# A Newton iteration for 32x32 inverses: sixteen small array tiles, or one whole array with masked, block-diagonal weights

## The chip, the cores and the metric

The kernel runs on one core of a Trainium2 chip. The metric is device time of one execution in microseconds, lower is better. Engines: TensorE (PE in the profile, PEld for its weight loads), VectorE (DVE), ScalarE (ACT), GpSimd (POOL), SyncE (SP).

## The reference

Nystrom attention on 8 batches of 8 heads (576 tokens, head size 64), then a multiplicative feed-forward layer on the 4608 resulting tokens:

```python
q_lm = q.reshape(B, H, m, S // m, D).mean(axis=3)         # m = 32 landmarks
A, Bm, C = sm(q, k_lm), sm(q_lm, k_lm), sm(q_lm, k)       # softmax of scaled products
Z = Bm.T / (norm1(Bm) * norminf(Bm) + 1e-6)               # per head, 32x32
for _ in range(6):
    Z = 2 * Z - Z @ Bm @ Z                                # iterative inverse
x = (A @ Z @ C @ v)                                       # heads side by side: 4608 x 512
out = ((x @ w1) * (x @ w2)) @ w3 @ w_out                  # 512 -> 1024 -> 1024 -> 512
```

## The kernel before, in words

**Stages.** The product w3 w_out is formed once on the chip (`w34`): w3 comes in eight row blocks of 128, each is turned on TensorE (`w3_tr`, tasks `tr`), split into a high and a low f16 part on ScalarE and VectorE (`w3_hi`, `w3_lo`), and multiplied with the equally split w_out (`w34_mm`, tasks `mm{j}{c}`, three matmuls each). w_out comes in eight pieces (`wf{c}`). Meanwhile the attention runs for "quads" of four heads (`quad_tasks`, sixteen of them): GpSimd loads q and k (`lq`), sums them to landmark means (`mean_a` to `mean_c`), VectorE transposes, TensorE makes the scores (tasks `S`, `A`), and so on. A pair of batches g (four pairs) then goes through the "lane" (`pair_tasks`): softmax of Bm and its norms (`ba` to `no`), five steps of the iteration (`x{g}_{i}`), a last product (`Z`), its spreading to a block-diagonal tile `zb` on VectorE (`z_out`, task `zo`), the product with C v (`W`), a split to f16 (`w_out`, task `wq`), and from there, for each of the two batches, the products with w1 and w2 (`U`). Last come the dense stages: `d` (192 columns, four matmuls of two heads' groups each) with their product on ScalarE and VectorE (`e`, `f`), and `g` (512 columns, four matmuls per task) with copy and store. The dense stages of one batch run on TensorE between the attention work of later ones.

**The iteration.** The tile `xz` holds, for 16 heads, X = I - Bm Z (part 0) and Z (part 1), head hb of four in partitions 32 hb to 32 hb + 31, and four groups s side by side. A step is X times (X, Z): for each of the 16 heads a 32x32 f32 weight tile and 64 moving columns, each at its own 32x32 place of the array (`it_mm`). Then ScalarE copies X X to the next tile (`it_sq`, task `v`), and VectorE adds X Z to Z (`it_out`, task `y`). The next step needs both.

**What sets the order.** `Plan` is a list scheduler that runs while the kernel is built. Each task has an engine, an assumed duration, dependencies, ring buffers that it takes (`acq`) and gives back (`rel`), a due time (`prio`) and for TensorE a mode, the array's tile shape. It starts, engine by engine, the task that can start first; on TensorE tasks within 0.05 us of that compete by due time, and one in the array's present mode has its due time moved ahead, by MP = 0.9 for the whole array and by MT for the small tile shapes. The result is a fixed order for each engine's in-order queue; only semaphores decide when things run. Due times follow from `dense(b) = T0 + 19.5 b`; `att(n)` for quads and `lane(g)` for the iteration are set off from it.

Names and lines that the text uses: line 239 is the helper `mm` (all plain matmuls), 310 the w_out load, 315 the w3 load, 333 the w3 transposes, 415 the q and k loads, 436 the w1 and w2 loads, 452 to 467 the landmark sums on GpSimd, 626 a normalisation on GpSimd, 815 `it_sq`, 824 `it_out`, 839 `z_out`, 859 and 860 `w_out`, 959 and 965 the dense product. `swapneg` is a constant 128x128 f32 matrix with which TensorE exchanges row maxima between partitions (`s_swap`, tasks `sw`). `bank` is any of six PSUM banks; buffers named `osb`, `ecT` and `u` also serve as landing places of weights at the start.

Of the kernel before, what the change touches and what calls it, by code (L numbers as in the profile page):

```python
# [11 lines left out]
ALU = mybir.AluOpType  # L12
AX = mybir.AxisListType

B = 8
# [7 lines left out]
DF = 1024  # L23
HALF = 288
MP = 0.9
MT = 12.0
THIRD = 192
NCH = 8
X64 = 64.0
# [12 lines left out]
class Plan:  # L42
# [15 lines left out]
    def add(self, name, eng, dur, fn, deps=(), acq=(), rel=(), prio=0.0, mode=None, lat=None,  # L58
            move=0.0, after=0.0):
        t = Task(name, eng, dur, fn, list(deps), list(acq), list(rel), prio, mode,  # L60
                 self.LAT[eng] + self.SLACK if lat is None else lat, move, after)
        self.by[name] = t
        self.tasks.append(t)
        return t
# [101 lines left out]
def kernel(  # L166
# [11 lines left out]
    nc = tc.nc  # L178
    P = Plan()
# [7 lines left out]
    def bank(i):  # L187
        return banks[i]
# [28 lines left out]
    xzs = slots(fixed, 3, [128, 4, 2, 32], FP32, "xz")  # L217
# [15 lines left out]
    def at(key, i=0):  # L233
        return P.slot[key][i]
# [3 lines left out]
    def mm(out_, lhsT, rhs, start=True, stop=True, pos=None):  # L238
        nc.tensor.matmul(out_, lhsT, rhs, start=start, stop=stop,  # L239
                         **({} if pos is None else {"tile_position": pos}))  # L240


    T0 = 66.0
    PER = 19.5

    def dense(b):
# [1 line left out]

    def att(n):
        first = dense(2 * (n // 4)) - 53.0 + 7.5 * (n % 4)  # L250
        return max(3.0 + 6.0 * n, first)

    def lane(g):
        return dense(2 * g) - 26.0
# [58 lines left out]
    def load_w3(j, c0=0, c1=DF):  # L313
        def fn():
            nc.sync.dma_start(out=w3n[at(f"w3n{j}")][:, c0:c1], in_=moe_w3[128 * j:128 * j + 128, c0:c1])
        return fn
# [45 lines left out]
    def w34_out(j):  # L362
# [2 lines left out]
                                 scale=1.0 / (WSC * WSC))  # L365
        return fn

    def w34_tasks():
        for j in range(8):
            p0 = 4.0 + 8.6 * j  # L370
            cuts = [(0, 1), (1, 4), (4, 8)] if j == 0 else [(0, 4), (4, 8)]
            acq = [("w3n", f"w3n{j}", 1, len(cuts))]
            if j == 0:
                for h, (c0, c1) in enumerate(cuts):
                    add(f"wm{h}" if h else "w3n0", "SP", 0.43, load_w3(0, 128 * c0, 128 * c1),
                        acq=[] if h else acq, prio=(-0.01, 0.105, 0.115)[h], move=0.183 * (c1 - c0), lat=2.0)
            else:
                add(f"w3n{j}", "SP", 0.43, load_w3(j), acq=acq, prio=0.125 if j == 1 else p0 - 8.0,
                    after=0.0 if j == 1 else max(0.0, p0 - 12.0), move=1.46, lat=2.0)
            if j == 0:  # L380
                for c in range(8):
                    add(f"wf{c}", "SP", 0.43, load_wout(c), acq=[("wf", f"wf{c}", 1, 2)],
                        prio=0.1 + 0.01 * c, move=0.73, lat=2.0)
                    add(f"woh{c}", "ACT", 0.53, wout_hi(c), deps=[f"wf{c}"], rel=[f"wf{c}"],
                        prio=1.0 + 0.1 * c)
                    add(f"wol{c}", "DVE", 0.62, wout_lo(c), deps=[f"wf{c}", f"woh{c}"],
                        rel=[f"wf{c}"], prio=1.0 + 0.1 * c)
            for h, (c0, c1) in enumerate(cuts):
                acq = [("P", f"ptr{j}{h}", 1, 2)]
                if h == 0:  # L390
                    acq.append(("w3t", f"w3t{j}", 1, 8))
                k = (c1 - c0) / 4
                add(f"tr{j}{h}", "PE", 0.44 * k, w3_tr(j, h, c0, c1),
                    deps=["cb", f"wm{h}" if h and j == 0 else f"w3n{j}"] + ([f"tr{j}{h - 1}"] if h else []), acq=acq,
                    rel=[f"w3n{j}"], prio=p0 - 4.0 + h, mode="full")
                add(f"wh{j}{h}", "ACT", 0.13 + 0.35 * k, w3_hi(j, h, c0, c1), deps=[f"tr{j}{h}"], rel=[f"ptr{j}{h}"],
                    prio=p0 - 3.5 + h)
                add(f"wl{j}{h}", "DVE", 0.1 + 0.51 * k, w3_lo(j, h, c0, c1), deps=[f"tr{j}{h}", f"wh{j}{h}"],
                    rel=[f"ptr{j}{h}"], prio=p0 - 3.5 + h)
            part = {c: h for h, (c0, c1) in enumerate(cuts) for c in range(c0, c1)}  # L400
            for c in range(8):
                deps = [f"woh{c}", f"wol{c}", f"wh{j}{part[c]}", f"wl{j}{part[c]}"]
                if c:
                    deps.append(f"mm{j}{c - 1}")
                add(f"mm{j}{c}", "PE", 0.65, w34_mm(j, c), deps=deps,
                    acq=[("P", f"pw{j}", 1, 1)] if c == 0 else [], rel=[f"w3t{j}"],
                    prio=p0 + 0.7 * c, mode="full")
            add(f"wo{j}", "ACT", 0.48, w34_out(j), deps=[f"mm{j}7"], rel=[f"pw{j}"], prio=p0 + 6.0)
# [391 lines left out]
    def it_mm(g, i):  # L800
        def fn():
            ps, xz = bank(at(f"pX{g}_{i}")), xzs[at(f"xz{g}_{i}")]
            for s in range(4):
                for hb in range(4):
                    r = slice(32 * hb, 32 * hb + 32)
                    mm(ps[r, 64 * s:64 * s + 64], xz[r, s, 0, :], xz[r, s, :, :],
                       pos=(32 * hb, 32 * hb))
        return fn

    def it_ps(g, i):  # L810
        return bank(at(f"pX{g}_{i}"))[:, 0:256].rearrange("p (s t x) -> p s t x", s=4, t=2)

    def it_sq(g, i):
        def fn():
            nc.scalar.copy(out=xzs[at(f"xz{g}_{i + 1}")][:, :, 0, :], in_=it_ps(g, i)[:, :, 0, :])  # L815
        return fn
# [10 lines left out]
    def z_mm(g):  # L827
        def fn():
            ps, xz = bank(at(f"pZ{g}")), xzs[at(f"xz{g}_5")]
            for s in range(4):  # L830
                for hb in range(4):
                    r = slice(32 * hb, 32 * hb + 32)
                    mm(ps[r, 32 * s:32 * s + 32], xz[r, s, 1, :], xz[r, s, 0, :],
                       pos=(32 * hb, 32 * hb))
        return fn
# [60 lines left out]
    def pair_tasks(g):  # L896
        p = lane(g)
        add(f"ba{g}", "DVE", 0.5, b_soft_a(g), deps=[f"bo{4 * g + i}" for i in range(4)],
            acq=[("tiny", f"tb{g}", 1, 2), ("P", f"pN{g}", 1, 1)], rel=[f"bsc{g}"], prio=p)
        add(f"bb{g}", "ACT", 0.25, b_soft_b(g), deps=[f"ba{g}"], prio=p + 0.3)  # L900
        add(f"bc{g}", "DVE", 1.08, b_soft_c(g), deps=[f"bb{g}"], acq=[("bm", f"bm{g}", 1, 1)],
            rel=[f"tb{g}"], prio=p + 0.6)
        add(f"N{g}", "PE", 0.52, norm_mm(g), deps=[f"bc{g}"], prio=p + 1.5, mode="32x32")
        add(f"no{g}", "DVE", 1.47, norm_out(g), deps=[f"N{g}"],
            acq=[("xz", f"xz{g}_0", 1, 2)], rel=[f"pN{g}", f"bm{g}", f"tb{g}"], prio=p + 2.0)
        last = [f"no{g}"]
        for i in range(5):
            add(f"x{g}_{i}", "PE", 0.46, it_mm(g, i), deps=last,
                acq=[("P", f"pX{g}_{i}", 1, 1 if i == 4 else 2), ("xz", f"xz{g}_{i + 1}", 1, 1 if i == 4 else 2)],
                rel=[f"xz{g}_{i}"], prio=p + 3.5 + 1.5 * i, mode="32x32")  # L910
            last = [f"y{g}_{i}"]
            add(f"y{g}_{i}", "DVE", 0.44 if i == 4 else 0.22, it_out(g, i), deps=[f"x{g}_{i}"],
                rel=[f"xz{g}_{i}", f"pX{g}_{i}"], prio=p + 3.8 + 1.5 * i)
            if i < 4:
                add(f"v{g}_{i}", "ACT", 0.24, it_sq(g, i), deps=[f"x{g}_{i}"], rel=[f"pX{g}_{i}"],
                    prio=p + 3.8 + 1.5 * i)
                last.append(f"v{g}_{i}")
        add(f"Z{g}", "PE", 0.28, z_mm(g), deps=last, acq=[("P", f"pZ{g}", 1, 1)], rel=[f"xz{g}_5"],
            prio=p + 11.0, mode="32x32")
        add(f"zo{g}", "DVE", 0.6, z_out(g), deps=[f"Z{g}"], acq=[("zb", f"zb{g}", 1, 1)],  # L920
            rel=[f"pZ{g}"], prio=p + 11.3)
        add(f"W{g}", "PE", 0.47, w_mm(g), deps=[f"zo{g}", f"co{2 * g}", f"co{2 * g + 1}"],
            acq=[("P", f"pY{g}", 1, 1)],
            rel=[f"zb{g}", f"cv{2 * g}", f"cv{2 * g + 1}"], prio=p + 12.0, mode="128x64")
        add(f"wq{g}", "DVE", 0.8, w_out(g), deps=[f"W{g}"], acq=[("wT", f"wT{g}", 1, 8)],
            rel=[f"pY{g}"], prio=p + 12.3)

    def u_tasks(b):
        p = dense(b) - UO
# [137 lines left out]
    for s in range(2):  # L1067
        for qd in range(2):
            for wi in range(2):
                add(f"lw{s}{qd}{wi}", "POOL", 0.62, load_w12(s, qd, wi), prio=T0 - 10.0 + qd, after=T0 - 10.0 - 4.0,  # L1070
                    move=1.46, lat=2.0)
    for n in range(NQ):
        quad_tasks(n)
# [54 lines left out]
```

## Time and profile before

| | |
|---|---|
| runs | 283.07 us median of 3 (281.07, 283.07, 283.90) |
| profiled execution | 281.59 us, its span 279.8 us |
| mean granted TensorE clock | 0.997 |
| instructions in the profile | 9998 |
| DMA | 37.34 MB moved, mean 133 GB/s |

The profile is one execution as the hardware profiler took it. Times are us from the span's start. In a line of a group stand: line, engine, operation, output and input tiles, shapes, count; then busy us in total and mean ns of one; then idle time of the engine just before these instructions, and what ended it. In a timeline a line is a run of like instructions: start, us from the first start to the last end, engine, line, operation, tiles, shape, count; in brackets the idle time before it and its releaser. A matmul's end is modelled and overlaps the next one's start, so for TensorE the distance between starts is what counts. One f32 matmul of the program shows as two records. The engines' busy time over the span (40 slices, tenths):

```profile
PE   3799999988999999999999899999999999999993
PEld 1456566744647767776676666756776665775762
DVE  2669995978858999779979757777883462442540
ACT  4643453424467776567986177599746667768551
POOL 8902999987998979989898920121010000000000
```

### The profile page before, as it was taken

What the parts mean: (1) busy time and instruction counts of PE and PEld (TensorE: products, weight loads), DVE (VectorE), ACT (ScalarE), POOL (GpSimd) and SP (SyncE); (2) the same over time, 40 slices, a digit from 0 to 9 for tenths busy, and PEclk for the clock granted to TensorE, in tenths of its full rate; (3) what the DMA queues carried; (4) which work ended last, traced back from release to release, by engine and by line L of the source; (5) the groups of instructions that cost most, each with busy time, mean ns of one, the idle gap of its engine ahead of it and who ended that gap; (6) DMA issues with size and microseconds to landing.
All of it is one profiled execution on the core that took longest, in us unless ns stands there. A gap on an engine that the chain in (4) does not pass through costs nothing.

```text
span 279.8 us, 9998 instructions
## 1 busy us (share of the span) xinstructions
PE 264.4 (94%) x4116; PEld 177.3 (63%) x4116; DVE 195.0 (70%) x514; ACT 167.2 (60%) x457; POOL 141.9 (51%) x183
## 2 busy tenths in 40 slices
PE   3799999988999999999999899999999999999993
PEld 1456566744647767776676666756776665775762
DVE  2669995978858999779979757777883462442540
ACT  4643453424467776567986177599746667768551
POOL 8902999987998979989898920121010000000000
PEclk9999999999999999999999999999999999999998
DMA  6999995999935564789832751211211112121223
GB/s 176 316 316 270 256 286 116 232 219 215 187 66 87 86 124 127 171 234 184 178 98 89 180 156 40 76 39 41 77 41 42 40 45 71 63 89 40 77 76 112
DMA packets 19181, 37.34 MB, mean 133 GB/s; under 512 B 2880, under 2 KB 3392, under 8 KB 19136
## 3 DMA queue, kind: packets, MB, share of 16 engines
q1 hardware_dynamic: 13136, 24.91, 29.3%
q0 software_dynamic: 5760, 11.54, 23.7%
q8 instruction: 32, 0.52, 0.8%
q10 hardware_dynamic: 240, 0.26, 0.3%
q14 instruction: 13, 0.11, 0.1%
HBM read 38.80 MB, written 9.44 MB: 172 GB/s over the span
## 4 chain that ended last, share of the span: by engine, by line
PE 80%; DVE 12%; DMA 2%; issue 2%; ACT 1%; SPq 1%; DVEq 0%
PE bank L239 73%; PE wide L239 4%; DVE ab L965 3%; DMA osb<-in_moe_w_dram 2%; PE bank L333 2%; DVE bank L747 1%; PE bank L635 1%; DVE tiny L598 1%; DVE ea L604 1%; DVE ecT L563 1%; DVE tiny L520 1%; DVE tiny L619 1%; DVE Tq L444 1%; DVE Tk L444 0%; SPq L310 0%
## 5 line engine op out<-in xcount | busy, mean ns | idle before, releaser
L239 PEld LDWEIGHTS <-u 128*128 128x128 f16 x960 | 81.3, 99 | 32.2 <-issue 8.1
L965 DVE TENSOR_TENSOR ab<-asb,bank 128x192 f16<-128x192 f16 x192 | 60.2, 347 | 38.4 <-ACT asb L959 37.9
L239 PE MATMUL bank<-aT,u 128*128 128x192 f16 x768 | 78.2, 247 | 0.3 <-DVE ab L965 0.3
L239 PE MATMUL bank<-w,ab 128*128 128x512 f16 (+1 forms) x296 | 73.4, 374 | 0.8 <-issue 0.8
L959 ACT CAST asb<-bank 128x192 f16<-128x192 f32 x192 | 57.5, 329 | 22.9 <-PE bank L239 19.4
L239 PE MATMUL bank<-wo,u 128*128 128x512 f16 x192 | 50.5, 395 | 0.0
L459 POOL TENSOR_TENSOR ls<-ls 128x128 f32<-128x128 f32 (+2 forms) x56 | 40.8, 728 | 3.6
L239 PEld LDWEIGHTS <-ab 128*128 128x128 f16 x296 | 26.9, 98 | 22.0 <-issue 3.8
L452 POOL TENSOR_TENSOR ls<-nat 128x1152 f32<-128x1152 f16 x14 | 33.3, 2382 | 12.5 <-DVE Tk L444 12.1
L881 ACT CAST u<-bank 128x512 f16<-128x512 f32 x64 | 35.2, 599 | 6.4 <-PE bank L239 6.2
L626 POOL TENSOR_TENSOR ah<-ea,tiny 128x512 f16<-128x512 f32 (+1 forms) x16 | 18.5, 1159 | 37.9 <-ACT u L881 16.5
L991 ACT ACTIVATE osb<-bank 128x512 f32<-128x512 f32 x35 | 21.2, 605 | 12.7 <-PE bank L239 12.5
L547 ACT ACTIVATE ec<-wide,tiny 128x288 f32<-128x288 f32 x32 | 15.8, 501 | 9.1 <-DVE tiny L540 9.0
L239 PE MATMUL bank<-w,wT 64*32 64x512 f16 x512 | 18.9, 380 | 0.0
L239 PE MATMUL bank<-vb,ecT 128*32 128x128 f32 x576 | 17.9, 273 | 0.0
L340 ACT ACTIVATE u<-bank 128x512 f16<-128x512 f32 (+2 forms) x17 | 9.7, 569 | 12.2 <-PE bank L333 8.5
L467 POOL TENSOR_TENSOR lm<-ls,meanS 128x256 f16<-128x256 f32 x28 | 16.6, 617 | 0.4
L239 PE MATMUL bank<-xz 32*32 32x64 f32 (+1 forms) x768 | 15.1, 213 | 1.6 <-DVE cv L737 1.4
L239 PEld LDWEIGHTS bank<-xz 32*32 32x32 f32 x768 | 11.2, 105 | 7.5 <-issue 2.4
L815 ACT COPY xz<-bank 128x128 f32<-128x128 f32 x16 | 4.3, 269 | 19.3 <-PE bank L239 19.1
L239 PEld LDWEIGHTS bank<-vb,ecT 128*32 128x32 f32 x576 | 15.7, 110 | 0.3 <-issue 0.2
L563 DVE STREAM_TRANSPOSE ecT<-ec 128x576 f32<-128x576 f32 x16 | 12.1, 756 | 3.6 <-ACT ec L547 3.6
(93 smaller groups left out, 325.2 us busy)
## 6 DMA issues: line engine op xcount, KB each, us to landing
vb<-in_v_dram SPq DMA_DIRECT2D x64, 144.0 KB, 5.0
out_dram<-osb SPq DMA_DIRECT2D x37, 128.0 KB, 2.3
nat<-in_k_dram POOLq DMA_DIRECT2D x16, 288.0 KB, 5.1
nat<-in_q_dram POOLq DMA_DIRECT2D x16, 288.0 KB, 7.0
out_dram<-osb SPq DMA_DIRECT2D x16, 256.0 KB, 3.0
w3n<-in_moe_w_dram SPq DMA_DIRECT2D x4, 512.0 KB, 10.9
w<-in_moe_w_dram POOLq DMA_DIRECT2D x8, 256.0 KB, 6.4
osb<-in_moe_w_dram SPq DMA_DIRECT2D x3, 512.0 KB, 6.9
```

The lines of the kernel that those rows point to most:

```text
L239: nc.tensor.matmul(out_, lhsT, rhs, start=start, stop=stop, **({} if pos is None else {"tile_position": pos}))
L340: nc.scalar.activation(out=w3t[at(f"w3t{j}")][:, 0, 128 * c0:128 * c1], in_=bank(at(f"ptr{j}{h}"))[:, 0:128 * (c1 - c0)], func=AXF.Copy, s ...
L452: nc.gpsimd.tensor_tensor(out=l, in0=nat[:, :, 0:9, :], in1=nat[:, :, 9:18, :], op=ALU.add)
L459: nc.gpsimd.tensor_tensor(out=l[:, :, x:x + m, :], in0=l[:, :, x:x + m, :], in1=l[:, :, y:y + m, :], op=ALU.add)
L467: nc.gpsimd.tensor_tensor(out=lm[:, 4 * t:4 * t + 4, :], in0=l[:, t, 0, :].unsqueeze(1).to_broadcast([128, 4, D]), in1=meanS.unsqueeze(2). ...
L547: nc.scalar.activation(out=ecs[at(f"ec{n}")][:, hp, :, :].rearrange("p c x -> p (c x)"), in_=psS[:, hp, 0:HALF], func=AXF.Exp, scale=SCALE ...
L563: nc.vector.transpose(out=ecTs[at(f"ecT{n}")].rearrange("p a c x -> p (a c x)"), in_=ecs[at(f"ec{n}")].rearrange("p a c x -> p (a c x)"))
L626: nc.gpsimd.tensor_tensor(out=ahs[at(f"ah{n}")][:, 0:g, :], in0=eas[at(f"ea{n}")][:, 0:g, :], in1=tinies[at(f"ta{n}")][:, 0:g].unsqueeze(2 ...
L881: nc.scalar.copy(out=uu[at(f"u{b}{qd}")][:, wi, 512 * half:512 * half + 512], in_=bank(at(f"pU{b}{wi}{half}{qd}")))
L959: nc.scalar.copy(out=asb[at(f"as{b}{j}{th}")], in_=bank(at(f"pD{b}{j}{th}"))[:, 0:THIRD])
L965: nc.vector.tensor_mul(ab[:, j, c0:c0 + THIRD], asb[at(f"as{b}{j}{th}")], bank(at(f"pD{b}{j}{th}"))[:, THIRD:2 * THIRD])
L991: nc.scalar.activation(out=osb[at(f"os{t}")], in_=bank(at(f"pE{t}")), func=AXF.Copy, scale=2.0 ** -12)
```

## The change

1. A step of the iteration uses the whole array. `it_diag`, new, spreads X to a block-diagonal 128x128 matrix for each group s: X repeated four times along the free dimension, times the mask `blockones`, into the tile `zb` (128 x 512 f32). `it_mm` then makes 4 matmuls per step, each with 128x128 weights from `zb` and 64 moving columns, instead of 16 with 32x32 weights.
2. The spreading runs on VectorE for pair 0, where from the second step on it reads X X from PSUM and does not wait for ScalarE's copy; for pairs 1 to 3 it runs on GpSimd, which reads the copy. `POOLX` says which.
3. The lane's due times are stretched (2.5 us a step on GpSimd, 1.8 on VectorE, 1.5 before), `zb` is taken at the first step instead of at `zo`, and the PSUM bank of a step on VectorE has one more user.
4. The first w3 block comes in one load instead of three (128, 384 and 512 columns), and the second block's load stands behind four w_out pieces instead of three.
5. MT goes from 12 to 6, T0 from 66 to 68, the floor in `att` from 3 + 6n to 9 + 6n, and the loads of w1 and w2 are due 16 instead of 10 before T0.

```diff
-MT = 12.0
+MT = 6.0
...
+    POOLX = [i >= int(1.0) for i in range(B // 2)]
...
-    T0 = 66.0
+    T0 = 68.0
...
-        return max(3.0 + 6.0 * n, first)
+        return max(9.0 + 6.0 * n, first)
...
+    W1 = 4.0
+    FIRST = [(0, 1), (1, 4), (4, 8)]
+    PIECES = [(0, 8)]
...
-                for h, (c0, c1) in enumerate(cuts):
+                for h, (c0, c1) in enumerate(PIECES):
                     add(f"wm{h}" if h else "w3n0", "SP", 0.43, load_w3(0, 128 * c0, 128 * c1),
-                        acq=[] if h else acq, prio=(-0.01, 0.105, 0.115)[h], move=0.183 * (c1 - c0), lat=2.0)
+                        acq=[] if h else acq, prio=-0.01 + h * 0.11, move=0.183 * (c1 - c0), lat=2.0)
             else:
-                add(f"w3n{j}", "SP", 0.43, load_w3(j), acq=acq, prio=0.125 if j == 1 else p0 - 8.0,
+                add(f"w3n{j}", "SP", 0.43, load_w3(j), acq=acq, prio=0.1 + 0.01 * W1 - 0.005 if j == 1 else p0 - 8.0,
...
     def it_mm(g, i):
         def fn():
             ps, xz = bank(at(f"pX{g}_{i}")), xzs[at(f"xz{g}_{i}")]
+            xd = zbs[at(f"zb{g}")]
             for s in range(4):
-                for hb in range(4):
-                    r = slice(32 * hb, 32 * hb + 32)
-                    mm(ps[r, 64 * s:64 * s + 64], xz[r, s, 0, :], xz[r, s, :, :],
-                       pos=(32 * hb, 32 * hb))
+                mm(ps[:, 64 * s:64 * s + 64], xd[:, s, :, :].rearrange("p h x -> p (h x)"), xz[:, s, :, :])
+        return fn
+
+    def it_diag(g, i):
+        def fn():
+            if POOLX[g]:
+                eng, src = nc.gpsimd, xzs[at(f"xz{g}_{i}")][:, :, 0, :]
+            else:
+                eng, src = nc.vector, it_ps(g, i - 1)[:, :, 0, :] if i else xzs[at(f"xz{g}_0")][:, :, 0, :]
+            eng.tensor_tensor(out=zbs[at(f"zb{g}")], in0=src.unsqueeze(2).to_broadcast([128, 4, 4, 32]),
+                              in1=blockones.rearrange("p (h x) -> p h x", h=4).unsqueeze(1)
+                              .to_broadcast([128, 4, 4, 32]), op=ALU.mult)
         return fn
...
         last = [f"no{g}"]
+        q = p + 3.5
         for i in range(5):
-            add(f"x{g}_{i}", "PE", 0.46, it_mm(g, i), deps=last,
-                acq=[("P", f"pX{g}_{i}", 1, 1 if i == 4 else 2), ("xz", f"xz{g}_{i + 1}", 1, 1 if i == 4 else 2)],
-                rel=[f"xz{g}_{i}"], prio=p + 3.5 + 1.5 * i, mode="32x32")
+            pool = POOLX[g]
+            acq = [("zb", f"zb{g}", 1, 1)] if i == 0 else []
+            if pool:
+                add(f"xm{g}_{i}", "POOL", 1.05, it_diag(g, i), deps=last[-1:], acq=acq, prio=q)
+            else:
+                add(f"xm{g}_{i}", "DVE", 0.6, it_diag(g, i), deps=last[:1] if i == 0 else [f"x{g}_{i - 1}"], acq=acq,
+                    rel=[f"pX{g}_{i - 1}"] if i else [], prio=q)
+            add(f"x{g}_{i}", "PE", 0.5, it_mm(g, i), deps=last + [f"xm{g}_{i}"],
+                acq=[("P", f"pX{g}_{i}", 1, 1 if i == 4 else 2 if pool else 3),
+                     ("xz", f"xz{g}_{i + 1}", 1, 1 if i == 4 else 2)],
+                rel=[f"xz{g}_{i}"], prio=q + 0.5, mode="full")
...
-                add(f"lw{s}{qd}{wi}", "POOL", 0.62, load_w12(s, qd, wi), prio=T0 - 10.0 + qd, after=T0 - 10.0 - 4.0,
+                add(f"lw{s}{qd}{wi}", "POOL", 0.62, load_w12(s, qd, wi), prio=T0 - 16.0 + qd, after=T0 - 16.0 - 4.0,
```

## The prediction

> **What bounds the kernel now.** I read the page's busy times and chain first, then busy time in ten-microsecond windows, then TensorE's timeline around the work that changes, then the groups kept apart by shape.
>
> ```profile
> PE 264.4 (94%) x4116; PEld 177.3 (63%) x4116; DVE 195.0 (70%) x514; ACT 167.2 (60%) x457; POOL 141.9 (51%) x183
> ...
> PE 80%; DVE 12%; DMA 2%; issue 2%; ACT 1%; SPq 1%; DVEq 0%
> ```
>
> TensorE is busy for 94% of the span and carries 80% of the chain that ended last. The windows say where it is not full (columns: stretch, length, then busy time and instructions of PE, PEld, DVE, ACT, POOL, then clock, DMA share, GB/s):
>
> ```profile
> 0.00:10.00 10.00, 3.89 (x12) 1.99 (x13) 4.36 (x23) 4.77 (x10) 8.90 (x14) 1.00 0.78 239
> ...
> 50.00:60.00 10.00, 8.52 (x216) 6.14 (x217) 9.40 (x24) 4.07 (x11) 9.41 (x13) 1.00 1.07 230
> 60.00:70.00 10.00, 8.85 (x177) 5.11 (x166) 7.75 (x19) 3.52 (x10) 6.98 (x12) 1.00 1.09 213
> ...
> 150.00:160.00 10.00, 8.71 (x243) 6.76 (x231) 8.81 (x29) 3.53 (x12) 9.29 (x11) 1.00 0.63 164
> ```
>
> Holes are 6.1 us in the first window, 1.5 and 1.2 where pair 0 iterates, 1.3 (and 0.6 in the next window) where pair 2 does. Everywhere else PE's column shows 9.5 to 10.0 of 10 until the last window, where stores drain, at a granted clock of 1.00. So a microsecond of TensorE work added anywhere is nearly a microsecond added to the end; work on the other engines costs only where it opens a hole.
>
> **TensorE: the iteration's shape.** One step today, and what follows it:
>
> ```profile
> 59.58 0.65 PE L239 MATMUL bank<-xz 32*32 32x64 f32 x32 [1.39 <-DVE cv L737]
> 60.16 0.82 PE L239 MATMUL bank<-wo,u 128*128 128x512 f16 x3
> ```
>
> The 16 f32 matmuls are 32 records (two passes each). The next matmul starts 0.58 us after the first. In that lie 0.49 us of matmuls (four blocks run side by side) and 0.09 us to change the array's tile shape: between single records, each undisturbed change of shape costs 0.09 us over the streaming time, whatever the two shapes.
>
> After the change a step is 4 matmuls on the whole array, 8 records, each with its own 128x128 f32 weight load. No iteration step shows that load, but the swap of the maxima (tile `swapneg`) does: two such loads, two moving columns each.
>
> ```profile
> 41.13 0.30 PEld L239 LDWEIGHTS wide<-tiny,swapneg 128*128 128x128 f32 x2 [0.43 <-DVE tiny L520]
> ...
> 41.13 0.38 PE L239 MATMUL wide<-tiny,swapneg 128*128 128x2 f32 x2
> 41.37 0.59 PE L239 MATMUL bank<-wo,u 128*128 128x512 f16 x2
> ```
>
> ```profile
> L239 PEld LDWEIGHTS wide<-tiny,swapneg 128*128 128x128 f32 x32 | 5.5, 190 | 2.2 <-DVE tiny L520 0.4 <-DVE xz L824 0.4 <-issue 0.2
> L239 PEld LDWEIGHTS bank<-xz 32*32 32x32 f32 x768 | 11.2, 105 | 7.5 <-issue 2.4 <-DVE cv L737 1.6 <-DVE ab L965 0.8
> ```
>
> Two loads of 0.19 us span 0.30, so the second starts 0.11 after the first, though the matmul between them streams next to nothing. The f16 matmul behind comes 0.24 after the first start. The load, not the 64 columns, sets the pace: 0.24 + 6 x 0.11 = 0.90 us for eight records when PE stood waiting. Behind a 512-column matmul the first load is hidden (at 68.56 the pair took 0.14 until the next start): 0.14 + 0.66 = 0.80. Behind a 192-column matmul the gap for two is 0.17: 0.83, which I take, since most steps follow such work. A step thus grows from 0.49 to 0.83 (0.80 to 0.90), and twenty steps by 20 x 0.34 = +6.8 us (+6.2 to +8.2).
>
> The Trainium skill, TensorE: Matmul & The Clock Gate, LDWEIGHTS and Weight-path perf modes, speaks against this change: a load takes its columns divided by 1.2 GHz, and the fast load is off for FP32. By that, as an estimate, a step is 8 x 107 ns = 0.85 us; the 0.11 us above agrees.
>
> In return the steps no longer need a small tile shape. In the two built orders the shape changes 141 times before and 115 times after (the lower stickiness MT included): 26 x 0.09 = -2.3 us. Numbers of all other TensorE tasks are equal. **TensorE's sum: +4.5 us (+3.9 to +5.9).**
>
> **The masks.** VectorE does five for pair 0, GpSimd fifteen for pairs 1 to 3.
>
> ```profile
> L839 DVE TENSOR_TENSOR zb<-bank,blockones 128x512 f32<-128x512 f32 x4 | 2.8, 688 | 0.4 <-PE bank L239 0.4
> ...
> L459 POOL TENSOR_TENSOR ls<-ls 128x512 f32<-128x512 f32 x14 | 17.9, 1275 | 0.3
> ...
> L626 POOL TENSOR_TENSOR ah<-ea,tiny 128x512 f16<-128x512 f32 x8 | 8.4, 1049 | 19.8 <-PE bank L239 11.9 <-DVE tiny L620 7.0 <-ACT asb L959 0.9
> ```
>
> VectorE: 5 x 0.69 = 3.4 us, the very operation of `z_out`. They fall at 52 to 72 us, where VectorE is busy 9.4 and 7.8 of 10 and PE already waits for it. The windows leave it 2.8 us, so I charge a hole of 1.0 us (0 to 3).
>
> GpSimd: f32 out is nearest L459, so 1.28 (1.05 at least); 15 x 1.28 = 19 us, ten of them before 175 us, where GpSimd is 9 of 10 busy. Each waits for ScalarE's copy, and queued behind it stand means, norms and q/k loads. Their users are far behind: quad 9's mean ended at 109.8 and its scores ran at 125.0, quad 15's at 162.9 and 189.8. Ten masks are 12.8 us, spread along that way: nothing. With the cover gone it would be the excess, one for one.
>
> **The chain of a step.** From matmul start to ScalarE's copy was 0.71 us (56.36 to 57.07), 0.22 beyond the 0.49; the copy takes 0.27. With a GpSimd mask: 0.83 + 0.22 + 0.27 + 1.28 + two handovers of 0.15 = 2.9 us; pair 0 on VectorE: 0.83 + 0.22 + 0.69 + 0.2 = 1.9. PE is in order, so what stands between two steps covers this. The built order puts 2.2 us at least between pair 3's steps (such as four 192-column groups of 0.33 and a 0.86), 3 to 4 us in pairs 1 and 2, 1.5 to 1.7 in pair 0; with the step's own 0.83 that is 3.0 and 2.3 or more. It just holds: nothing, bounds -2 (other holes close) to +2. At the end of the lane cover is thin: W1 to the first U of batch 2 was 8.8 us in the trace, and the order now leaves two 0.33 groups, 0.14 and 0.86 there (1.7), against about 1.2 for `w_out` and its handovers.
>
> **The start.** PE was full only from 9.85, released by this transfer:
>
> ```profile
> 3.57 6.24 DMA osb<-in_moe_w_dram
> ```
>
> One load replaces three, so SP issues two fewer of 0.43 to 0.47 us. But the second w3 block now stands behind four w_out pieces, not three: 256 KB more. From 4.67 to 9.81, 1280 KB landed, 249 KB per us: +1.0 later, less about 0.5 for fewer issues and longer rows. PE meanwhile does the three matmuls of the second chunk early (0.65). Sum 0 (-0.7 to +0.8). The eight w1/w2 loads (0.62 each of GpSimd) now all stand ahead of quad 5's mean, which ended at 64.5 for scores at 75.5: covered, 4.9 us if it were not. The floor 9+6n never exceeds the other term of att. T0 + 2 only moves targets.
>
> **Sum** against the profiled execution of 281.59 (span 279.81): 4.5 + 1.0 = +5.5, so 287.1. The median of the runs, 283.07, lies 1.5 above it; on its scale 288.6.
>
> **Rivals.**
> 1. The load hides behind streaming. A record would then cost 0.056 as in today's waves, a step 0.45 to 0.49, and only the -2.3 remains (to -3.1): 280.4, faster. For: four f32 transposes with 128x128 weights take 0.44, and f16 loads hide wholly. Against: the 0.11 between loads. It decides where a record costs under 0.08 (26 x 0.09 / 20 + 0.49 = 0.61 per step). Chance 15%.
> 2. Holes close. The new order has different waits; if half of the 11 us of holes that precede 170 us goes, the growth is paid: 283. For: the holes come from order. Against: VectorE gets more work just there. 12%.
> 3. The lane becomes the bound: PE stands at each GpSimd step and at U because masks queue behind 2.4 us sums on GpSimd. At 0.3 per step, 15 x 0.3 = 4.5 more: 293. It decides where the chain exceeds 3.0 us. For: cover is under 0.2 us in pair 3. 11%.
> 4. Loads don't overlap streaming at all: 0.11 + 0.056 per record, a step 1.33, so 20 x 0.84 - 2.3 + 1.0 = +15.5: 298.6. Against: f16 groups of four 192-column matmuls keep 0.33, and `zb,cv` alternates f32 loads and streams at streaming pace. 4%. The Trainium skill, TensorE: Matmul & The Clock Gate, Part 3, The mechanism, has loads overlap in-flight matmuls only when the row group differs (or into a background buffer); the full array is one group, so its first half gives this rival, and the trace sides with the second.
>
> That the change isn't done can be put aside: the built order shows 20 steps of four 128-row matmuls, 5 masks on VectorE and 15 on GpSimd.
>
> **Numbers.** My case has 58%: +1.9 (3.9 - 2) to +9.7 (5.9 + 3 + 0.8), 285.0 to 292.8. One per cent is 2.8 us, about what the spread of the runs (281.07 to 283.9) lets one tell. My case is slower by more with .50 and within with .08; rivals 3 and 4 add .15 slower; rival 1 splits .08 faster, .07 within; rival 2 .05 faster, .05 within, .02 slower. So faster .13, same .20, slower .67. The range 282.5 to 292.7 leaves out rival 1, rival 4 and the ends.
>
> **What would show it.** `xz,zb` loads near 0.19 us and 0.11 apart, steps of 0.80 to 0.90 until the next start: right. Steps near 0.5: rival 1. PE busy up by about 4.5 us and holes within 1 or 2 us of before: my sum. PE waiting before each step of pairs 1 to 3: rival 3. The first full stretch of PE at about 9.9; GpSimd masks near 1.28 and VectorE's near 0.69.

## The result, and the profile after

The changed kernel took 282.38 us (median of 20 runs, 281.66 to 287.27). The kernel before, run 20 times on the same chips, took 281.50. The ratio is 1.005, 95% interval 1.0028 to 1.0072: half a per cent slower, too little to matter and far less than the 5.5 us that were forecast. The profiled execution took 282.38 us (before 281.59), its span 280.5 us (279.8).

TensorE still carries the time. The profile's first part and its chain by engine, after:

```profile
PE 266.4 (95%) x3636; PEld 184.7 (66%) x3636; DVE 196.5 (70%) x519; ACT 167.1 (60%) x457; POOL 160.2 (57%) x198
...
PE 72%; POOL 14%; DMA 7%; DVE 3%; issue 2%; ACT 1%; POOLq 0%
```

VectorE's share of the chain fell from 12% to 3%. GpSimd, which was not in it, and DMA, which had 2%, now hold 21%. The ten-microsecond windows of the changed kernel (stretch, length, busy time and instructions of PE, PEld, DVE, ACT, POOL, then clock, DMA share, GB/s) show where:

```profile
0.00:10.00 10.00, 5.16 (x21) 3.17 (x22) 4.52 (x14) 5.20 (x9) 8.90 (x14) 1.00 0.78 282
10.00:20.00 10.00, 8.27 (x62) 4.78 (x61) 7.59 (x23) 5.45 (x14) 4.31 (x8) 1.00 1.08 298
20.00:30.00 10.00, 8.62 (x87) 4.97 (x85) 8.00 (x17) 2.79 (x7) 3.37 (x3) 1.00 1.10 271
30.00:40.00 10.00, 9.23 (x104) 5.87 (x105) 8.74 (x16) 5.56 (x13) 9.68 (x13) 1.00 1.05 279
...
50.00:60.00 10.00, 10.00 (x172) 7.00 (x171) 9.00 (x24) 3.82 (x10) 8.21 (x16) 1.00 1.02 217
60.00:70.00 10.00, 9.80 (x98) 7.50 (x98) 8.33 (x20) 3.43 (x9) 8.08 (x10) 1.00 1.11 247
...
150.00:160.00 10.00, 9.38 (x174) 7.17 (x172) 8.57 (x27) 4.78 (x16) 7.75 (x9) 1.00 0.48 140
```

In the three windows of the lane that stood in the prediction, PE's holes were 1.48, 1.15 and 1.29 us (3.9 together). They are now 0, 0.20 and 0.62 (0.8). The first window's hole fell from 6.1 to 4.8 us, but 3.9 us of new ones opened at 10 to 40 us, where before PE's column showed 10.00. The step itself, on TensorE's timeline of the changed kernel (start, length, line, operation, tile, shape, count):

```profile
59.10 0.81 PE L239 MATMUL bank<-wo,u 128*128 128x512 f16 x3
59.75 1.00 PE L239 MATMUL bank<-xz,zb 128*128 128x64 f32 x8
60.59 0.59 PE L239 MATMUL bank<-wo,u 128*128 128x512 f16 x2
```

From the step's first start to the next matmul's are 0.84 us, against 0.58 with the change of shape before. And the groups, after:

```profile
L239 PEld LDWEIGHTS bank<-xz,zb 128*128 128x128 f32 x160 | 20.1, 191 | 2.0 <-POOL zb L820 0.5 <-issue 0.4 <-DVE zb L820 0.2
L820 POOL TENSOR_TENSOR zb<-xz,blockones 128x512 f32<-128x512 f32 x15 | 19.0, 1270 | 14.5 <-ACT xz L830 12.0 <-DVE xz L800 2.4
L820 DVE TENSOR_TENSOR zb<-bank,blockones 128x512 f32<-128x512 f32 x4 | 2.7, 686 | 0.3 <-ACT xz L830 0.3
L753 DVE TENSOR_TENSOR bank<-bsc,tiny 128x128 f32<-128x128 f32 x4 | 2.5, 613 | 0.3
```

Loads at 191 ns, masks at 1270 and 686 ns: all three prices were right. The last row is the subtraction of row maxima at the head of the lane. It isn't part of the change and comes up below.

**Where TensorE's time went.** For each run the distances between matmul starts were put into five bins: streaming; the excess at a change of tile shape, up to 0.09 us; the steps' own matmuls; lost at the start (to the first matmul, half-rate matmuls, and waits up to 45 us); and waits after 45 us, with half-rate matmuls there. Streaming and the last products are alike in all kernels within 0.5 us. The bins, in us, are those of one profiled execution each. Its own time stands beside the median, and the two differ by up to 2 us:

| kernel | median | ratio to before (95%) | profiled | steps | shape | lost to 45 us | waits after 45 us |
|---|---|---|---|---|---|---|---|
| before | 281.50 | | 281.59 | 10.0 | 12.9 | 11.2 | 7.5 |
| after | 282.38 | 1.005 (1.0028 to 1.0072) | 282.38 | 17.3 | 10.5 | 11.5 | 2.9 |
| e1_form_only | 284.22 | 1.0064 (1.0030 to 1.0098) | 284.10 | 17.5 | 10.4 | 11.0 | 5.1 |
| e2_form_undone | 283.42 | 1.0034 (1.0001 to 1.0068) | 284.34 | 9.8 | 13.0 | 11.9 | 9.4 |
| e3_loads_only | 281.39 | 0.9985 (0.9955 to 1.0015) | 280.26 | 10.0 | 13.3 | 11.2 | 5.5 |
| e4_knobs_only | 280.88 | 0.9961 (0.9929 to 0.9993) | 280.28 | 10.3 | 13.2 | 11.3 | 5.4 |
| e5_nl_form_undone | 277.53 | 0.9853 (0.9829 to 0.9877) | 277.58 | 9.8 | 13.0 | 11.3 | 3.8 |
| e6_nl_after | 281.21 | 0.9988 (0.9957 to 1.0018) | 280.88 | 17.3 | 10.5 | 11.5 | 1.7 |
| e7_nl_before | 281.24 | 0.9982 (0.9951 to 1.0013) | 279.24 | 10.0 | 12.9 | 11.4 | 5.0 |
| e8_nl_form_only | 283.61 | 1.0071 (1.0046 to 1.0095) | 283.75 | 17.5 | 10.4 | 11.6 | 4.2 |
| e9_nl_stretch | 280.13 | 0.9935 (0.9907 to 0.9963) | 280.48 | 10.0 | 13.1 | 11.6 | 5.3 |
| e10_nl_old_due | 281.31 | 0.9971 (0.9947 to 0.9995) | 281.91 | 17.3 | 10.5 | 12.1 | 1.8 |
| e11_nl_all_dve | 287.34 | 1.0162 (1.0125 to 1.0199) | 288.21 | 17.5 | 10.8 | 12.1 | 7.5 |
| e12_nl_split_cols | 299.94 | 1.0617 (1.0564 to 1.0670) | 299.84 | 34.7 | 10.5 | 11.3 | 3.2 |
| e13_nl_mask_32 | 278.42 | 0.9891 (0.9849 to 0.9932) | 279.53 | 9.8 | 13.8 | 11.6 | 4.2 |
| e14_nl_form_mode32 | 283.36 | 1.0057 (1.0028 to 1.0086) | 284.90 | 17.3 | 10.6 | 12.3 | 4.9 |
| e15_nl_loads_only | 279.10 | 0.9910 (0.9878 to 0.9942) | 278.26 | 10.0 | 13.3 | 11.7 | 3.1 |

From before to after: steps +7.3, shape -2.4, start +0.4, waits after 45 us -4.7; together +0.6, where the start of the last matmul moved by +0.5. So the TensorE work came as forecast, and waits that closed after 45 us paid for it. The question was why.

### The profile page after: what moved, and what is told of

The parts are those of the page before. It is cut to its first block, busy times and chain, and to the rows that moved or that the text cites. A ratio compares the mean times of both kernels' runs of the same rounds, so it can differ in the third digit from the quotient of the medians.

```text
span 280.5 us, 9068 instructions
## 1 busy us (share of the span) xinstructions
PE 266.4 (95%) x3636; PEld 184.7 (66%) x3636; DVE 196.5 (70%) x519; ACT 167.1 (60%) x457; POOL 160.2 (57%) x198
## 4 chain that ended last, share of the span: by engine, by line
PE 72%; POOL 14%; DMA 7%; DVE 3%; issue 2%; ACT 1%; POOLq 0%
PE bank L239 67%; DMA nat<-in_q_dram 5%; PE wide L239 3%; POOL ls L465 3%; POOL vb L298 3%; POOL ls L458 3%; POOL nat L421 2%; DMA w<-in_moe_w_dram 2%; POOL ah L632 2%; PE bank L641 1%; POOL lm L473 1%; DVE ab L989 1%; DVE bank L753 1%; PE bank L335 0%; ACT osb L1015 0%
## 5 line engine op out<-in xcount | busy, mean ns | idle before, releaser
L989 DVE TENSOR_TENSOR ab<-asb,bank 128x192 f16<-128x192 f16 x192 | 59.0, 347 | 35.9 <-ACT asb L983 35.1
L239 PE MATMUL bank<-aT,u 128*128 128x192 f16 x768 | 77.4, 246 | 0.4 <-DVE ab L989 0.4
L458 POOL TENSOR_TENSOR ls<-nat 128x1152 f32<-128x1152 f16 x14 | 33.4, 2385 | 12.5 <-DMA nat<-in_q_dram 12.3
L896 ACT CAST u<-bank 128x512 f16<-128x512 f32 x64 | 34.6, 603 | 6.7 <-PE bank L239 6.0
L1015 ACT ACTIVATE osb<-bank 128x512 f32<-128x512 f32 x35 | 21.5, 613 | 11.8 <-PE bank L239 11.1
L820 POOL TENSOR_TENSOR zb<-xz,blockones 128x512 f32<-128x512 f32 x15 | 19.0, 1270 | 14.5 <-ACT xz L830 12.0
L239 PEld LDWEIGHTS bank<-xz,zb 128*128 128x128 f32 x160 | 20.1, 191 | 2.0 <-POOL zb L820 0.5
L239 PE MATMUL bank<-xz,zb 128*128 128x64 f32 x160 | 20.6, 272 | 0.0
L239 PE MATMUL bank<-vb,ecT 128*32 128x128 f32 x576 | 17.5, 273 | 0.0
L619 ACT ACTIVATE ea<-ea 128x512 f32<-128x512 f32 (+1 forms) x16 | 11.2, 701 | 9.9 <-DVE ea L610 9.8
L342 ACT ACTIVATE u<-bank 128x512 f16<-128x512 f32 (+2 forms) x17 | 9.6, 567 | 11.4 <-PE bank L335 11.4
L651 ACT COPY aT<-bank 128x512 f16<-128x512 f16 x16 | 9.5, 593 | 10.4 <-PE bank L641 10.4
## 6 DMA issues: line engine op xcount, KB each, us to landing
w<-in_moe_w_dram POOLq DMA_DIRECT2D x8, 256.0 KB, 11.6
```

Of the source, the lines that this page charges most:

```text
L239: nc.tensor.matmul(out_, lhsT, rhs, start=start, stop=stop, **({} if pos is None else {"tile_position": pos}))
L458: nc.gpsimd.tensor_tensor(out=l, in0=nat[:, :, 0:9, :], in1=nat[:, :, 9:18, :], op=ALU.add)
L619: nc.scalar.activation(out=ea, in_=ea, func=AXF.Exp, scale=SCALE)
L820: eng.tensor_tensor(out=zbs[at(f"zb{g}")], in0=src.unsqueeze(2).to_broadcast([128, 4, 4, 32]), in1=blockones.rearrange("p (h x) -> p h x", ...
L896: nc.scalar.copy(out=uu[at(f"u{b}{qd}")][:, wi, 512 * half:512 * half + 512], in_=bank(at(f"pU{b}{wi}{half}{qd}")))
L989: nc.vector.tensor_mul(ab[:, j, c0:c0 + THIRD], asb[at(f"as{b}{j}{th}")], bank(at(f"pD{b}{j}{th}"))[:, THIRD:2 * THIRD])
```

## The experiments

### The parts by themselves

The change has three parts: the form of the step with its masks and due times (1 to 3 of the change), the loads of w3 (4), and the planner's numbers (5). e1 has the first alone, e2 all but the first, e3 and e4 the other two alone. The edits are hunks of the change put back; that of e2 and of e1:

```diff
# e2: form undone (also it_diag, its tasks and the lane's due times)
-                mm(ps[:, 64 * s:64 * s + 64], xd[:, s, :, :].rearrange("p h x -> p (h x)"), xz[:, s, :, :])
+                for hb in range(4):
+                    r = slice(32 * hb, 32 * hb + 32)
+                    mm(ps[r, 64 * s:64 * s + 64], xz[r, s, 0, :], xz[r, s, :, :], pos=(32 * hb, 32 * hb))
...
# e1: loads and planner's numbers as before (e3 and e4 undo the form and one of these)
-    W1 = 4.0
-    PIECES = [(0, 8)]
+    W1 = 3.0
+    PIECES = FIRST
...
-    MT = 6.0
-    T0 = 68.0
+    MT = 12.0
+    T0 = 66.0
```

> The kernel before with the array form alone (block-diagonal masks, four matmuls a step, the lane's new due times); the loads of w3 and MT, T0, att and the w1/w2 due time as before. Theory S (the parts add up): the form costs its TensorE work, +7.3 us of steps less 2.5 us of shape changes (114 instead of 141), so about +4.9 us, 286.4; holes as before, about 7.7 us after 20 us. Rival R (the form pays for itself, because whole-array steps let holes around the lane close): +1.5 us or less, 283.0, holes after 20 us near 5.4.

> The changed kernel with the array form taken back (sixteen 32x32 matmuls a step, no masks, the lane's old due times), w3 loads and MT, T0, att, w1/w2 as changed. Theory S: the changed kernel's time less 4.9 us: 277.5, the fastest so far. Rival R: within 1.5 us of the kernel before, 280 to 283.

> The kernel before with the w3 loads alone changed (first block in one load, the second behind four w_out pieces). Theory S: TensorE's start is worth -2.0 us (half-rate matmuls 3.3 to 1.4 us, waits 4.9 to 3.4, first matmul 1.4 later), so 279.5. Rival R: nothing beyond 0.5 us, because a later wait takes it back: 281.5.

> The kernel before with MT 6, T0 68, att floor 9 and the earlier w1/w2 loads alone. Theory S: the closing of holes after 20 us is theirs: -2.3 us, 279.2. Rival R: the holes close through the form, these do nothing: 281.0 to 282.0.

Measured: +0.64%, +0.34%, -0.15% and -0.39%. e3 came out as by R; e1 and e4 lie between their two cases. The single parts add to +0.10%, the whole is +0.50%. That miss of 0.4% is within the noise of four ratios. e2 misses by more: loads and numbers together should be -0.54% and are +0.34%, 2.5 us off. Neither theory had that: by S the parts add up, by R the form closes holes and pays for itself. e2 lost most of it in one place. The windows of e2 around 100 us (columns as above):

```profile
100.00:102.00 2.00, 0.00 (x0) 0.00 (x0) 2.00 (x1) 0.00 (x0) 2.00 (x2) 0.98 1.00 200
102.00:104.00 2.00, 1.14 (x6) 0.81 (x6) 2.00 (x5) 1.02 (x4) 1.84 (x3) 0.50 0.15 54
104.00:106.00 2.00, 2.00 (x24) 0.85 (x26) 1.90 (x9) 0.61 (x2) 1.76 (x4) 0.50 0.00 0
```

For 2 us TensorE runs nothing, VectorE one instruction and GpSimd two; then TensorE's clock is 0.50, by the trace's record of the clock from 101.92 to 108.75, for 6.8 us. VectorE's timeline of e2 names the one instruction:

```profile
98.52 0.28 DVE L750 TENSOR_REDUCE tiny<-bsc 128x4 f32<-128x128 f32 x1
98.90 3.65 DVE L751 TENSOR_TENSOR bank<-bsc,tiny 128x128 f32<-128x128 f32 x1
102.47 0.60 DVE L969 TENSOR_TENSOR ab<-asb,bank 128x192 f16<-128x192 f16 x2
```

and GpSimd's timeline of e2 shows what ran meanwhile:

```profile
98.66 1.27 POOL L630 TENSOR_TENSOR ah<-ea,tiny 128x640 f16<-128x640 f32 x1
99.88 0.20 POOL L559 TENSOR_TENSOR tiny<-tiny,maskS 128x4 f32<-128x4 f32 x1
100.04 2.35 POOL L456 TENSOR_TENSOR ls<-nat 128x1152 f32<-128x1152 f16 x1
102.46 2.07 POOL L463 TENSOR_TENSOR ls<-ls 128x512 f32<-128x512 f32 x2
```

The subtraction of the row maxima, at the head of the lane, has 128 elements per partition. It stood from 98.90 to 102.55, over three GpSimd instructions, and ended 0.16 us after the landmark sum did. Of the lines shown it is the only one of VectorE's with two inputs in SBUF (`bsc` and the maxima in `tiny`). The product behind it (L969) fed TensorE, which stood 3.2 us.

### The collision taken away

If two SBUF inputs are the cause, one input in PSUM must end it. The "nl" kernels put the four maxima of a row into a free corner of a PSUM bank that the lane holds anyway; everything else, the planner's order too, stays:

```diff
-            nc.vector.reduce_max(out=t[:, 0:4], in_=bsc, axis=AX.X)
+            mx = bank(at(f"pN{g}"))[:, 128:132]
+            nc.vector.reduce_max(out=mx, in_=bsc, axis=AX.X)
             nc.vector.tensor_tensor(out=ps, in0=bsc,
-                                    in1=t[:, 0:4].unsqueeze(2).to_broadcast([128, 4, 32]),
+                                    in1=mx.unsqueeze(2).to_broadcast([128, 4, 32]),
```

Four kernels got it: e2 (as e5), the whole change (e6), the kernel before (e7), and e1 (e8).

> The changed kernel with the array form taken back, and the lane's first subtraction reading its maxima from PSUM instead of SBUF (one SBUF input in place of two), order of instructions the same. Theory C (what the sum missed is mostly this one VectorE instruction, which stood 3.6 us at 98.9 behind GpSimd's sums in the run before, and the half-rate matmuls after it): the instruction takes about 0.30 us four times out of four, TensorE's waits between 100 and 125 us fall from 5.4 to under 1, and the time from 283.4 to about 279. Rival D (something else on VectorE or GpSimd is as late, so the wait moves to the next instruction): 282.5 to 283.5, the waits stay above 3 us.

> The changed kernel with the same edit of the first subtraction. Theory C: there it stood 1.4 us in pair 2 alone, so -0.5 to -1: 281.5 to 282.0, and 2.5 to 3.5 us slower than the changed kernel with form and subtraction both edited (e5): the form costs nearly its TensorE work of 4.9 once the collisions are gone. Rival D: no faster than the changed kernel, within 1.5 us of e5.

> The kernel before with the same edit of the first subtraction (which took 0.98, 1.34, 0.91 and 0.37 us there). Theory C: each 0.30, TensorE's waits at 100 to 125 and 148 to 180 us down by about 1.5 together, the time -1 to -1.5: about 280. Rival D: unchanged within 0.5.

> The kernel before with the array form alone and the same edit of the first subtraction (1.27, 1.03, 0.30 and 0.30 us without the edit). Theory C: the difference to e7 is then the form by itself, +4 to +5 us, so 284 to 285. Rival D: as without the edit, +1.8 us over the kernel before, and holes go on closing by 2 us or more when the form is added.

The group of the subtraction, by instructions (minimum, median, maximum in ns; first and last start), in e2:

```profile
L751 DVE TENSOR_TENSOR bank<-bsc,tiny x4: 301/888/3649, 49.7 to 206.4; 128x128 f32<-128x128 f32 x4
```

and in e5:

```profile
L752 DVE TENSOR_TENSOR bank<-bsc,bank x4: 295/296/296, 49.2 to 199.7; 128x128 f32<-128x128 f32 x4
```

The one that took 3.65 us in e2 takes 0.295 in e5, from 98.85 to 99.14, although GpSimd runs the same instructions at the same time (the normalisation `ah` from 98.64 to 99.92, the landmark sum from 100.01 to 102.39). In all four kernels the subtraction takes 0.295 to 0.297 us every time. e5 takes 277.53 us where e2 took 283.42, 5.9 less, and waits after 45 us fell by 5.6, from 9.4 to 3.8. e5 is the fastest kernel of the study, 1.5% below before. The Trainium skill has this rule (SBUF — State Buffer, Who interferes with whom): a VectorE instruction with two SBUF inputs contends with a GpSimd instruction that reads SBUF, as an exclusive lock in which the one that comes second is blocked for the whole of the other instruction. The trace agrees that they contend, with 0.30 against 3.65 us for the same instruction; the block lasted longer than one GpSimd instruction, though, over three.

The other three kernels moved less. e6 came to 281.21, where theory C had 281.5 to 282.0. e7 came to 281.24 where it had 280, and its ratio, 0.9982, has an interval that holds 1; its profiled execution is the fastest of its twelve runs, so its bins show fewer waits than a typical run has. e8's ratio is no lower than e1's.

The new masks have it too. On VectorE a pair's first mask reads two SBUF tiles (`xz`, `blockones`). It took 0.68 us in the changed kernel. In e1 and e8 it met a landmark sum of GpSimd and took 1.83 and 2.45. That is luck of the order, not of the form.

With the subtraction's collision gone the form still doesn't cost its 5 us of TensorE work: e6 is 3.7 us above e5, where theory C had 2.5 to 3.5, and e8 2.4 above e7, where it had 4 to 5. The whole change makes no difference (281.24 to 281.21), though waits after 45 us fall from 5.0 to 1.7. So the collision was only a part of the closed holes: by the bins 2.5 us of the 7.5 before (7.5 - 5.0), 1.2 of the 2.9 after, hence 1.3 of the 4.7. The time bears out less of it, since the medians of before and e7 differ by 0.2%.

### What closed the other holes

Three causes were left: the stretched due times, the order that the planner finds for a step that needs no change of shape, and the wider step itself, which fills time that would else be a wait. e9 is e5 with the new due times; e10 is e6 with the old ones:

```diff
# e9: sixteen 32x32 matmuls as before, the lane's due times as after the change
-                rel=[f"xz{g}_{i}"], prio=p + 3.5 + 1.5 * i, mode="32x32")
+                rel=[f"xz{g}_{i}"], prio=q + 0.5, mode="32x32")
...
# e10: the changed form, the lane's due times as before it
-                rel=[f"xz{g}_{i}"], prio=q + 0.5, mode="full")
+                rel=[f"xz{g}_{i}"], prio=q, mode="full")
...
-            q += 2.5 if pool else 1.8
+            q += 1.5
```

> e5_nl_form_undone (32x32 steps, new loads and times, maxima in PSUM: 277.53) with one thing from the changed form: the lane's stretched due times (2.5 us per step for pairs 1 to 3, 1.8 for pair 0, in place of 1.5). No mask, no full array. Theory T (it is the due times that closed the lane's holes): TensorE's waits between 45 and 180 us fall from 3.1 us by 1.5 to 2.5, time 275.0 to 276.0. Rival F (it is the wider step itself, more TensorE work in the same place, that filled them): waits stay within 0.5 of 3.1, time 277.0 to 278.0.

> e6_nl_after (the whole change, maxima in PSUM: 281.21) with the lane's old due times (1.5 us per step). Theory T: the waits of the lane come back, from 1.9 us between 45 and 180 us (of it 1.2 after 45 us in the first pairs) to 3.5 or more, time 282.7 or more. Rival F: waits within 0.5, time 280.7 to 281.7. A third result, waits far above (over 5 us), would mean that a step with a GpSimd mask needs the 2.5 us, as the prediction's chain of 2.9 us has it.

Both speak against the due times alone as the cause. e10 changes nothing (281.31, waits 1.8). e9 went the other way than either theory said: 2.6 us slower than e5, with waits of 5.3 in place of 3.8 us, spread over six places of 0.3 to 0.9 us. Same instructions, another order, 2.6 us.

e13 keeps the order of e6, with all its masks, and puts the narrow step back. e14 keeps the wide step, and the planner is told that it needs the small shape:

```diff
# e13: it_mm as before the change, nothing else
-                mm(ps[:, 64 * s:64 * s + 64], xd[:, s, :, :].rearrange("p h x -> p (h x)"), xz[:, s, :, :])
+                for hb in range(4):
+                    r = slice(32 * hb, 32 * hb + 32)
+                    mm(ps[r, 64 * s:64 * s + 64], xz[r, s, 0, :], xz[r, s, :, :], pos=(32 * hb, 32 * hb))
# e14
-                rel=[f"xz{g}_{i}"], prio=q + 0.5, mode="full")
+                rel=[f"xz{g}_{i}"], prio=q + 0.5, mode="32x32")
```

> e6_nl_after (281.21) with TensorE's steps as before the change (sixteen 32x32 matmuls, waves of four), in the changed order and with all 20 masks still made and waited for. Steps fall by 7.3 us (17.3 to 10.0), and up to 40 changes of shape come in at 0.09 (the planner does not know of them): net -3.7 or a little more in TensorE's work. If TensorE's work is all that the form costs: 277.0 to 278.0. If the wide step filled holes that the masks' chain would otherwise leave (the filling theory): waits between 45 and 180 us rise from 0.9 to 2.5 or more and the time is 279 to 281.

> e6_nl_after (281.21) where the planner is told that a step needs the small tile shape, as before the change; the instructions are the same, their order is not. If it is the free placing (no change of shape to pay) that closed the lane's holes: waits between 45 and 180 us go from 0.9 to 2.5 or more, and 282.5 or more. If not: waits within 0.5 of 0.9, 280.7 to 281.7 plus whatever real changes of shape the new order adds (each 0.09).

e13 lies between its two cases: steps -7.5, shape +3.3, so 4.2 us less work, but 2.8 us less time (by the ratios 0.97%, 2.7 us). Waits after 45 us rose from 1.7 to 4.2. So with one order and the same masks the wide step does fill holes, 1.4 us by the medians and 2.5 in the two traces. Such a place on TensorE's timeline of e13:

```profile
65.38 0.45 PE L641 MATMUL bank<-ident,ah 128*128 128x128 f16 x5 [1.05 <-POOL ah L632]
66.41 0.65 PE L239 MATMUL bank<-xz 32*32 32x64 f32 x32
```

and on that of e6:

```profile
63.68 0.44 PE L641 MATMUL bank<-ident,ah 128*128 128x128 f16 x5
64.61 1.03 PE L239 MATMUL bank<-xz,zb 128*128 128x64 f32 x8
```

The bracket is the wait. GpSimd's normalisation `ah` is what both need, and its start moves too: 62.15 in e6 and 64.05 in e13, behind loads that wait for earlier loads to land. One trace each can't say how much of that place is the step and how much the loads.

e14 is 2.1 us slower than e6 by medians, as the theory of the free order had it. But 2.3 of its 4.9 us of waits are at one place, the same transposes of `ah`, and the steps themselves hardly wait. So another order was some 2 us worse in both cases (by the ratios 0.8% for e9 and 0.7% for e14), and why the planner's order was good here is not settled.

### The prices

e11 puts all masks on VectorE, e12 splits each matmul of a step into two of 32 columns with the same weights. Both start from e6.

```diff
# e11
-    POOLX = [i >= int(1.0) for i in range(B // 2)]
+    POOLX = [False for i in range(B // 2)]
# e12
-                mm(ps[:, 64 * s:64 * s + 64], xd[:, s, :, :].rearrange("p h x -> p (h x)"), xz[:, s, :, :])
+                for c in range(2):
+                    mm(ps[:, 64 * s + 32 * c:64 * s + 32 * c + 32], xd[:, s, :, :].rearrange("p h x -> p (h x)"),
+                       xz[:, s, c, :])
```

> e6_nl_after (281.21) with the 15 masks of pairs 1 to 3 on VectorE too. GpSimd loses 15 x 1.27 = 19.0 us, VectorE gains 15 x 0.69 = 10.3 us. If masks are covered on either engine (the prediction's view): 280.7 to 281.7. If VectorE is near its limit at 52 to 170 us: holes there and 282.5 to 285. If GpSimd's masks hold up what follows them: faster than 280.5.

> e6_nl_after (281.21) with each of the 80 matmuls of the steps split into two of 32 columns with the same block-diagonal weights: as many columns stream, twice as many weight loads. If the load sets the pace of a step (0.112 us per record, the prediction's step 2): 160 more records, +17.9 us of TensorE work, about 299. If streaming sets it (rival 1's premise): no more than +1, about 282. Records near 0.112 apart in the first case, near 0.056 in the second.

e12 settles the step's price. TensorE's timeline of e12:

```profile
56.92 1.87 PE L239 MATMUL bank<-xz,zb 128*128 128x32 f32 x16
58.62 0.81 PE L239 MATMUL bank<-wo,u 128*128 128x512 f16 x3
```

Sixteen records take 1.70 us to the next start, 0.106 each, with half the columns. The steps rose by 17.4 us, the time (of two runs) by 18.7. The load sets the pace, not the columns.

e11 was 6.1 us slower, more than the middle case allowed. Waits after 45 us are 7.5 us, and about half of that is one place, again the collision, now of a mask. VectorE's timeline of e11:

```profile
158.22 2.69 DVE L821 TENSOR_TENSOR zb<-xz,blockones 128x512 f32<-128x512 f32 x1
160.83 0.16 DVE L742 RECIPROCAL tiny<-bank 128x2 f32<-128x2 f32 x1
```

GpSimd's landmark sum ran from 157.99 to 160.36. The mask, 0.68 us by itself, ended 0.55 us after it. TensorE stood 1.73 us, and a window of e11 then shows the clock halved (the number ahead of the DMA share), by the record of the clock from 161.70 to 165.11:

```profile
162.00:163.00 1.00, 1.00 (x4) 0.49 (x4) 0.50 (x3) 0.27 (x1) 0.84 (x3) 0.50 1.01 249
```

So e11 doesn't tell what a covered VectorE mask costs. In this order GpSimd was the better place for pairs 1 to 3: a mask there stands in the same queue as GpSimd's sums and can't collide with them.

### The loads by themselves, without the collision

e15 is e7 with the new loads of w3 (the hunk of part 4), to see which part makes e5 fast.

> The kernel before with the new loads of w3 alone and the maxima in PSUM. e7_nl_before gave 281.24 and e5_nl_form_undone (new loads and new times) 277.53. If the loads make the gain: 277.5 to 278.5. If the planner's times do: 280.5 to 281.5.

279.10, between the two cases, 0.7% below e7 by the ratios. Lost time up to 45 us is 11.7, no better than 11.4. The gain is again in waits after 45 us (5.0 to 3.1): the loads change the order of what follows, not the start. In the two windows of pair 0, PE's holes are 0.3 us in e15 and 2.0 in e7, both with the narrow step. So the wide step isn't needed to close them. e15 is also e3 with the maxima in PSUM: by the ratios 0.75% less time (0.9985 to 0.9910), and e3 has 2.2 us of holes in those windows. What the collision costs thus depends on the order: 1.8% from e2 to e5, 0.75% here, 0.6% from the changed kernel to e6, 0.2% from before to e7.

## Why the prediction was wrong

The forecast was 288.6 us, 282.5 to 292.7. Measured were 282.38. Step by step:

- **The bound** held where work was merely added: e12 has 17.4 us more of steps and takes 18.7 us more. For the change itself "nearly a microsecond" was too much: some 5 us of TensorE work cost 2.4 us (e7 to e8) and 3.7 (e5 to e6).
- **TensorE's sum, +4.5 (3.9 to 5.9)**: right, +4.9. Steps +7.3 against +6.8, shape -2.4 against -2.3. A step is 0.84 to the next start, a record 0.11. Rivals 1 and 4 fall by e12 and by that pace.
- **The masks' own durations** were right (1.27 and 0.69). Their cover held on GpSimd: in the row of the step's weight loads, above, 0.5 us in all were spent waiting for its masks.
- **"I charge a hole of 1.0 us (0 to 3)", with bounds of -2 to +2 for other holes: the step that failed.** Waits after 45 us went from 7.5 to 2.9 us, -4.7. In the windows of pair 0, where the hole was to open, holes went from 2.6 to 0.2 us. The prediction set five masks, 3.4 us, against 2.8 us that VectorE had free there. All five ran there, yet VectorE was hardly busier than before (17.3 us of 20 against 17.2), because other work of its own had moved out, and TensorE was full between the steps. Of the 4.7, the bins give 1.3 to the collision of the subtraction (e6 and e7) and some 1.4 to 2.5 to filling by the wider step (e13). The remainder is order and isn't settled; the shares needn't add up either, as e15 closes pair 0's holes with the narrow step. That holes close was rival 2, with 283 and a chance of 12%. Its direction and its time came true, but not its count: the windows ahead of 170 us had 11.1 us of holes and still have 9.5, since new ones opened at 10 to 40 us.
- **The chain of a step, 2.9 us**, fitted: with a GpSimd mask, steps start 3.07 us apart or more. Rival 3 fell. Shorter due times (e10) made no difference.
- **The start, 0**: the number fits, +0.4, by luck, for its terms were others. In the kernel before, TensorE ran at half rate up to 15.1 us, although the windows' clock column shows 1.00 there: matmuls of 512 columns stood 0.43 us apart until then and 0.22 after. After the change this ended at 7.6 us, which saved some 2 us that the prediction has no term for, and the first window's hole shrank by 1.3. As much came back in waits that before had none of: 1.6 us at 15.0 for VectorE's low part `u`, 1.6 at 30.2 for GpSimd's normalisation and 0.5 at 33.3 for VectorE's `ea`. That is also the larger part of why PE's busy time rose by 2.0 us and not by 4.5: matmuls at half rate count as busy. All 17 kernels lose 11 to 12.3 us up to 45 us, whatever the loads are.
- **The scale**: the median of three runs, 283.07, was taken as 1.5 above the profiled execution. Twenty runs put it at 281.50. Of the miss of 6.2 us that is 1.5. The rest is the holes: -4.7 against +1.0 is 5.7 us, less 0.4 each for TensorE's sum and the start, which came out above. That makes 4.9, for the 4.7 between 287.1 and the profiled 282.38.

What could have been seen: the row of the subtraction in the profile of before.

```profile
L747 DVE TENSOR_TENSOR bank<-bsc,tiny 128x128 f32<-128x128 f32 x4 | 3.6, 900 | 0.2
```

Other instructions of 128x128 f32 take 290 ns there. A mean of 900 is 2.4 us of VectorE standing still in the lane, and the chain of before carries it with 1%. This row, three times as long as its likes, was not a cost of work but of something it waited for, and with another order its mean was 613 (after) and the longest one 3.65 us (e2).

## What to carry to other kernels

Compare mean durations of like shapes before costing a change: an instruction three times too long can be a hidden wait (here two SBUF inputs against GpSimd, ended by putting one input into PSUM), and what it costs depends on the order. Work added to the bounding engine costs what it adds less the holes it fills, so let the range of the holes reach down by as much as there are; here 4.7 of 7.5 us went. And undo parts of a change together as well as alone: the change hid that loads and planner's numbers, without the form and without the collision, make 277.53 us.

## What was not expected of the hardware

- A blocked VectorE instruction let three GpSimd instructions pass (98.66 to 102.39 in e2), not just the one that ran when it came: 3.65 us instead of 0.30. At 149.4 in the changed kernel it was only one, and 1.41 us.
- TensorE's clock fell to 0.50 in a wait of 3.2 us in e2, for 6.8 us, but also just after shorter ones, for 3.4 us each: 1.71 us in e5 (at 15.8), 1.73 in e11 and 1.89 in e14 (at 30.7). It stayed at 1.00 after 1.71 us in e13 (at 15.7), 2.1 in e14 (at 65.8) and 2.3 in e15. So 0.30 us of VectorE work cost TensorE a wait of 3.2 us and 6.8 us at half rate (e2). The Trainium skill (TensorE: Matmul & The Clock Gate, What's actually happening) has the gate look at a free-running window of 3.4 us, and close after an idle one. Half rate for 3.4 and 6.8 us, one window and two, agrees, and so does a wait of 1.71 us that trips it in one run and not in another. That so short a wait is enough differs from the page. No run shows where the windows lay.
- The same instructions in another order, all by the same planner, differ by 2.1 and 2.6 us (medians of e6 and e14, e5 and e9), as much as the parts of this change.
